# Chunked linear attention with two expert layers: the decay of the queries, the gate and ScalarE's late work are moved

## The chip, the cores and the metric

One core of a Trainium2 chip runs the whole program. The metric is the device time of one execution in microseconds (us). The engines are named as in the profile: PE is TensorE (PEld its weight loads), DVE is VectorE, ACT is ScalarE, POOL is GpSimd, SP is SyncE, which issues most DMAs.

## What is computed

Three layers follow one another: a linear attention with a decaying state, a mixture of eight experts with a greedy assignment under a capacity, and a dense layer of three products with a maximum. Only the attention and the gate's logits (`x @ w_gate`) bear on the change.

```python
def _attn_ref(r, k, v, w, u):                      # B, H, S, D = 4, 8, 768, 48
    for t in range(S):
        cur = einsum('bhd,bhe->bhde', u[None] * kt, vt)
        y[:, :, t] = einsum('bhd,bhde->bhe', rt, state + cur)
        state = w[None, :, :, None] * state + einsum('bhd,bhe->bhde', kt, vt)
def _moe_ref(x, w_gate, w1, w2):                   # 3072 tokens, 384 wide, 8 experts
    logits = x @ w_gate
    # greedy by logit, 384 tokens for each expert
    out[mask] = np.maximum(x[mask] @ w1[e], 0.0) @ w2[e]
# then: np.maximum(np.maximum(x @ v1, x @ v2), x @ v3) @ w_out
```

## The kernel before

The attention runs in 24 steps, one for each chunk of 128 tokens of one sequence: `steps` goes over the 6 chunks c, and inside over the 4 sequences b, so a sequence comes back every fourth step. Within a chunk the recurrence is turned into products: keys and queries are scaled by powers of the decay, the masked scores give the part of the chunk itself, and the state S of the sequence gives the part of the chunks before. Heads go in pairs, at partitions 0 to 47 and 64 to 111.

The order of the work is written out by hand in `Attention.run`: each engine takes its instructions in the order in which the program issues them. Step i issues, in this order: the loads for step i+4 (`load`), the transposed queries for i+3 (`across`), the storing of x of i-1 (`store`), all on SyncE's queue; GpSimd's decay of the queries of i+2 (`decayed`, L128, by the table `tr` in SBUF), its scaled keys of i+3 (`natural`, L183), its bonus products of i+2 (`bonus`, L191 and L192); then `turn` of i+2 (TensorE turns the keys, L212, ScalarE copies them out as `kt`, L214); `scores` of i+1 (TensorE L226, masked by VectorE as `am`, L229); `extra` of i+1 (VectorE sums the bonus, L200, GpSimd multiplies, L202); `cross` of i-1 (TensorE turns x into the bank `pX`, L297, ScalarE copies it out as `xt`, L299); `keep` (four products of constants, L236, whose result nobody reads); `rows` of i (TensorE L247, first against the state, then against the scores; VectorE adds the bonus into x, L262; ScalarE's Square of x with a sum, L263); `gate` of i-2 (three products with xt as the held operand, 8 columns, into 24 x 8 logits of one bank, L307); `state` of i (TensorE L281, VectorE's sum with the state, L285, and four copies by ScalarE that decay it, L289).

Between these lie four slots, `side(1)` to `side(4)`, in which the planner `Feed` issues the preparation of the expert weights: peaks by ScalarE's Square (L610), powers of two on VectorE, splits of each weight block into two half-precision parts by ScalarE (L677, L773) and VectorE (L681, L776), and the conversion of doubles (L717 to L748). The planner spreads its total cost evenly over the steps. What it has left is issued after the last step. Then the logits are negated into `raw` (L352), and the assignment of tokens and the expert products follow.

PSUM is full in this stage: one bank each for pT (turned keys), pX (x turned, also lent to the planner's small products), pK (state) and the logits, two each for pA (scores) and pY (rows).

Of the kernel before, what the change touches and what calls it, by code (L numbers as in the profile page):

```python
# [7 lines left out]
F32 = mybir.dt.float32  # L8
F16 = mybir.dt.float16
BF16 = mybir.dt.bfloat16  # L10
I32 = mybir.dt.int32
AF = mybir.ActivationFunctionType
# [6 lines left out]
C = 128  # L19
# [15 lines left out]
APART = 1.5  # L35
SLACK = (3.0, 2.0, 1.05, 2.0)
WARM = (20, 5, 14, 18)
KEEP = 4


def ap(t, offset, dims):
    return bass.AP(tensor=t.tensor, offset=t.offset + offset, ap=dims)


class Attention:


    def __init__(self, ctx, tc, K, r, rt, k, v, w, u, wg, x_dram, spare, routing):
        self.spare, self.routing = spare, routing
        self.tc, self.nc, self.K = tc, tc.nc, K  # L50
        self.r, self.rt, self.k, self.v, self.x_dram = r, rt, k, v, x_dram
        nc = self.nc
        self.loads = ctx.enter_context(tc.tile_pool(name="loads", bufs=5))
        self.work = ctx.enter_context(tc.tile_pool(name="work", bufs=2))
        self.tabs = ctx.enter_context(tc.tile_pool(name="tabs", bufs=1))
        self.psum = ctx.enter_context(tc.tile_pool(name="psum_a", bufs=1, space=PSUM))
        self.steps = [(b, c) for c in range(NC) for b in range(B)]
        self.LD, self.RN, self.KN, self.BV, self.RT, self.KT, self.AM, self.X, self.XT, self.RK = ({} for _ in range(10))
        wcol = self.tabs.tile([128, NP], F32, name="wcol")
        nc.vector.memset(wcol, 1.0)  # L60
        for s in range(2):
            nc.sync.dma_start(wcol[HALF[s]], ap(w, s * D, [[1, D], [R2, NP]]))
        self.RB, self.KB, self.KP = ([self.tabs.tile([128, NP * C], F32, name=f"{name}{j}") for j in range(m)]
                                     for name, m in (("rt", 4), ("kt", 2), ("kp", 4)))
        self.S = [self.tabs.tile([128, NP, WIDE], F32, name=f"S{b}") for b in range(B)]
        self.VB = [self.tabs.tile([128, DM + WIDE - D], F32, name=f"v{n}") for n in range(5)]
        nc.gpsimd.memset(self.RB[0], 0.0)
        self.load(0)
        self.across(0)
        for t in self.VB:  # L70
            nc.vector.memset(t[:, DM:], 0.0)
        self.K.identity()
        self.clear(self.KP[0])
        for t in self.RB[1:]:
            nc.gpsimd.memset(t, 0.0)
        for t in self.S:
            nc.gpsimd.memset(t[:, :, D:], 0.0)
        self.routing.fill()
        self.ub = self.tabs.tile([128, DM], F32, name="ub")
        nc.sync.dma_start(self.ub, ap(u, 0, [[0, 128], [1, DM]]))  # L80
        self.load(1)
        self.across(1)
        self.load(2)
        self.across(2)
        self.wg = self.tabs.tile([128, 3, E], F32, name="wg")
        nc.sync.dma_start(self.wg, ap(wg, 0, [[E, 128], [128 * E, 3], [1, E]]))
        self.tables(wcol)
        self.natural(1)
        self.natural(2)
        self.bonus(1)  # L90
        for i in range(2):
            self.decayed(i, nc.vector)
        self.bonus(0, nc.vector)
        self.fading()
        self.bank = self.psum.tile([128, 512], F32, name="lg")
        self.lg = self.bank[:, :NT * E].rearrange("p (m e) -> p m e", e=E)
        nc.tensor.matmul(self.bank[:, 256:], self.K.onesf.bitcast(BF16)[:, :128], self.K.onesf.bitcast(BF16), start=True, stop=True,
                         skip_group_check=True)

    def clear(self, t):  # L100

# [21 lines left out]
        for s in range(2):  # L123
            self.nc.sync.dma_start(t[HALF[s]], ap(self.rt, (b * NC + c) * C * DM + s * D * NP * C, [[NP * C, D], [1, NP * C]]))

    def decayed(self, i, engine=None):
        if i < NT:
            (engine or self.nc.gpsimd).tensor_mul(self.RT[i], self.RT[i], self.tr)  # L128

    def tables(self, wcol):  # L130
        nc, tabs, psum = self.nc, self.tabs, self.psum
        self.mask = tabs.tile([128, C], F32, name="mask")
        nc.gpsimd.memset(self.mask, 1.0)
        nc.gpsimd.affine_select(self.mask, self.mask, [[1, C]], OP.is_gt, 0.0, base=0, channel_multiplier=-1)
        scratch = [self.spare() for _ in range(2)]
        up, dn = (t[:, :NP * 65].rearrange("p (j n) -> p j n", n=65) for t in scratch)
        tk = scratch[0][:, 512:512 + NP * C].rearrange("p (j n) -> p j n", n=C)
        self.tr = tabs.tile([128, NP * C], F32, name="tr")
        tr = self.tr.rearrange("p (j n) -> p j n", n=C)
        nc.vector.memset(up[:, :, 0:1], 1.0)  # L140
        nc.vector.memset(dn[:, :, 64:65], 1.0)
        nc.vector.tensor_copy(up[:, :, 1], wcol)
        nc.vector.tensor_copy(dn[:, :, 63], wcol)
        pw = [wcol]
        n = 1
        while n < 64:
            p2 = tabs.tile([128, NP], F32, name=f"pw{2 * n}")
            nc.vector.tensor_mul(p2, pw[-1], pw[-1])
            b = pw[-1][:, :, None].to_broadcast([128, NP, n])
            nc.vector.tensor_mul(up[:, :, n + 1:2 * n + 1], up[:, :, 1:1 + n], b)  # L150
            nc.vector.tensor_mul(dn[:, :, 64 - 2 * n:64 - n], dn[:, :, 64 - n:64], b)
            pw.append(p2)
            n *= 2
        self.tkn = tabs.tile([128, H, 64], F32, name="tkn")
        for t in self.KP[1:]:
            self.clear(t)
        nc.scalar.activation(tk[:, :, :64], dn[:, :, 1:], AF.Copy)
        idle = psum.tile([128, 512], F32, name="pX")
        warm(nc, self.K, idle, WARM[0])
        for j in range(0, NP, 2):  # L160
            nc.vector.reciprocal(tk[:, j:j + 2, 64:], up[:, j:j + 2, 1:])
            p = psum.tile([128, 512], F32, name="pT")
            for n in range(2):
                nc.tensor.transpose(p[:, n * C:(n + 1) * C], tk[:, j + n, :], self.K.identf)
            warm(nc, self.K, idle, WARM[1])
            heads = slice(2 * j, 2 * j + 4)
            nc.scalar.activation(self.tkn[:, heads].rearrange("p h n -> p (h n)"), p[:, :2 * C], AF.Copy)
            self.natural(0, heads)
        nc.scalar.activation(tr[:, :, 64:], up[:, :, :64], AF.Copy)
        nc.vector.reciprocal(tr[:, :, :64], dn[:, :, :64])  # L170
        self.w64 = pw[-1]
# [57 lines left out]
            nc.vector.tensor_mul(am[:, s], pa[s], self.mask[:, None, :].to_broadcast([128, NP, C]))  # L229
        self.AM[i] = am  # L230

    def keep(self, n):

        ones = self.K.onesf.bitcast(BF16)
        for _ in range(n):
            self.nc.tensor.matmul(self.bank[:, 256:], ones[:, :128], ones, start=False, stop=True, skip_group_check=True)  # L236

    def rows(self, i):

        nc, psum = self.nc, self.psum  # L240
# [19 lines left out]
        parts = [t.rearrange("p (j s d) -> p j s d", j=NP, s=2) for t in (x, self.BV[i])]  # L260
        for s in range(2):
            nc.vector.tensor_add(parts[0][:, :, s], py[s][:, :, :D], parts[1][:, :, s])  # L262
        nc.scalar.activation(self.K.junk[:, :DM], x, AF.Square, accum_out=self.K.norms[:, i:i + 1])  # L263

    def store(self, i):
        if i >= 0:
# [4 lines left out]
    def state(self, i):  # L271
# [13 lines left out]
            nc.vector.tensor_add(t, pk[:, :, :D], S[:, :, :D])  # L285
        else:
            t = pk
        for j in range(NP):
            nc.scalar.activation(S[:, j, :D], t[:, j, :D], AF.Copy, scale=self.w128[:, j:j + 1])  # L289

    def cross(self, i):
        if i < 0:
            return
        nc, psum, work = self.nc, self.psum, self.work
        px = psum.tile([128, 3, C], F32, name="pX")
        for j in range(3):
            nc.tensor.transpose(px[:, j, :], self.X[i][:, j * 128:(j + 1) * 128], self.K.identf)  # L297
        xt = self.XT[i] = work.tile([128, 3, C], F32, name="xt", bufs=3)
        nc.scalar.activation(xt, px, AF.Copy)  # L299

    def gate(self, i):
        if i < 0:
            return
        b, c = self.steps[i]
        m = b * NC + c
        for j in range(3):
            self.nc.tensor.matmul(self.lg[:, m, :], self.XT[i][:, j, :], self.wg[:, j, :],  # L307
                                  start=(i == 0 and j == 0), stop=j == 2, skip_group_check=True)

    def run(self, feed):  # L310
        nc = self.nc
# [6 lines left out]
        for i in range(NT):  # L318
# [8 lines left out]
            self.load(i + 4)  # L327
            self.across(i + 3)
            self.store(i - 1)
            self.decayed(i + 2)  # L330
            self.natural(i + 3)
            self.bonus(i + 2)
            side(1)
            self.turn(i + 2)
            side(2)
            self.scores(i + 1)
            self.extra(i + 1)
            side(3)
            self.cross(i - 1)
            self.keep(KEEP)  # L340
            self.rows(i)
            self.gate(i - 2)
            side(4)
            self.state(i)
        while feed.left(9):
# [2 lines left out]
        self.gate(NT - 2)  # L348
        self.cross(NT - 1)
        self.gate(NT - 1)  # L350
        K = self.K
        nc.scalar.activation(K.raw, self.lg, AF.Copy, scale=-1.0)  # L352


class Consts:
# [1131 lines left out]
```

## Time and profile before

| | us |
|---|---|
| median of 3 runs | 698.33 |
| lowest and highest | 697.42, 699.98 |
| the profiled execution | 696.23 |
| its span in the profile | 694.5 |
| PE, DVE, ACT, POOL busy in the span | 644.6, 400.7, 351.5, 238.0 |

The busy times are sums over stages of very different kinds. The attention stage takes about the first 160 us, the assignment of tokens the 40 us after it, the expert and dense products the rest. So the page's totals say little of this change; views that are cut to the stage say more. In a waits view each row tells which engine and tile stood for which other engine and tile, in total, how often, and the longest. A busy PE includes short stalls inside a run of matmuls, since the ends of matmuls are modelled.

### The profile page before, as it was taken

How to read it: one execution, taken by the hardware profiler on the slowest of the kernel's cores; microseconds unless marked ns; L12 is line 12 of the kernel's file. 1: busy time of each engine (PE TensorE's matmuls, PEld its weight loads, DVE VectorE, ACT ScalarE, POOL GpSimd, SP SyncE). 2: the span in 40 equal slices, each digit the busy share in tenths (PEclk: the TensorE clock that was granted, in tenths of full speed). 3: DMA queues.
4: the chain of work that ended last, by engine and by line, in shares of the span. 5: the costliest groups of instructions: out<-in, count | busy, mean ns of one | idle time of the engine just before them, and what ended most of it. 6: DMA issues, size and time to landing. Idle time of an engine off the chain costs nothing.

```text
span 694.5 us, 14402 instructions
## 1 busy us (share of the span) xinstructions
PE 644.6 (93%) x5663; PEld 427.2 (62%) x5663; DVE 400.7 (58%) x1068; ACT 351.5 (51%) x785; POOL 238.0 (34%) x264
## 2 busy tenths in 40 slices
PE   7999998996599998699999999999999999999996
PEld 5788777875476554356666656666665666666663
DVE  7778897776725867646466455644636553451321
ACT  3766657643425556367466547446365536342321
POOL 6999999960050003113022112102212111110222
PEclk8999999995579999899999999999999999999999
DMA  7996757513034516016235211620612220000000
GB/s 220 315 295 216 246 186 250 162 37 103 2 107 139 172 42 194 22 68 160 68 103 108 98 57 30 170 75 35 160 45 74 45 89 1 35 0 1 36 1 34
DMA packets 54762, 72.97 MB, mean 105 GB/s; under 512 B 21408, under 2 KB 42016, under 8 KB 54688
## 3 DMA queue, kind: packets, MB, share of 16 engines
q1 hardware_dynamic: 51616, 62.55, 29.3%
q0 software_dynamic: 3072, 9.44, 4.7%
q8 instruction: 46, 0.75, 0.5%
q14 instruction: 28, 0.23, 0.1%
HBM read 58.41 MB, written 9.44 MB: 98 GB/s over the span
## 4 chain that ended last, share of the span: by engine, by line
PE 54%; issue 8%; DVE 5%; ACT 4%; POOL 1%; POOLq 0%; DVEq 0%; ACTq 0%
PE pg L897 25%; PE ps L897 20%; PE px L990 8%; ACT w L677 1%; DVE top L972 1%; POOL gt L977 1%; ACT junk L610 1%; DVE da L739 1%; DVE x2s L953 0%; ACT gt L976 0%; DVE ht L925 0%; DVE v L776 0%; DVE sc L423 0%; DVE da L732 0%; POOL out_dram L995 0%
## 5 line engine op out<-in xcount | busy, mean ns | idle before, releaser
L897 PE MATMUL pg<-x2s,v 128*128 128x384 f16 x1296 | 218.2, 326 | 5.3 <-ACT top L970 3.2
L897 PEld LDWEIGHTS <-v 128*128 128x128 f16 x1296 | 126.6, 98 | 90.9 <-issue 6.0
L977 POOL TENSOR_TENSOR gt<-top,gt 128x384 f16<-128x384 f32 x48 | 44.5, 928 | 349.2 <-ACT gt L976 295.5
L897 PEld LDWEIGHTS <-w 128*128 128x128 f16 x1242 | 116.8, 98 | 73.7 <-issue 2.3
L681 DVE SCALAR_TENSOR_TENSOR w<-stage,sc,w 128x512 f16<-128x512 f32 (+1 forms) x80 | 70.9, 906 | 61.1 <-ACT w L677 60.9
L972 DVE SCALAR_TENSOR_TENSOR top<-pg,sc,top 128x384 f32<-128x384 f32 x96 | 59.1, 615 | 74.4 <-PE pg L897 63.6
L897 PE MATMUL ps<-ht,w 128*128 128x384 f16 x576 | 94.9, 326 | 1.6 <-DVE ht L925 1.6
L897 PE MATMUL ps<-xt,w 128*128 128x384 f16 (+1 forms) x540 | 88.4, 317 | 0.2 <-ACT xt L888 0.2
L990 PE MATMUL px<-wo,gt 128*128 128x384 f16 x432 | 75.0, 334 | 6.9 <-DVE wo L776 3.0
L976 ACT ACTIVATE gt<-top 128x384 f16<-128x384 f32 x48 | 25.1, 523 | 109.5 <-DVE top L972 109.5
L990 PEld LDWEIGHTS <-gt 128*128 128x128 f16 x432 | 42.7, 100 | 38.1 <-issue 8.8
L677 ACT ACTIVATE w<-stage,sc 128x512 f16<-128x512 f32 (+1 forms) x80 | 61.6, 798 | 2.2 <-DVE sc L461 2.2
L610 ACT ACTIVATE junk<-stage 128x768 bf16<-128x768 f32 x64 | 53.7, 838 | 0.9
L925 DVE SCALAR_TENSOR_TENSOR ht<-ps,ht 128x384 f16<-128x384 f32 x56 | 31.0, 555 | 32.1 <-ACT ht L924 32.1
L995 POOL DMA_INDIRECT out_dram<-o,ids x24 | 23.9, 996 | 46.7 <-ACT o L993 46.7
L970 ACT ACTIVATE top<-pg,sc 128x384 f32<-128x384 f32 x48 | 27.6, 576 | 20.8 <-PE pg L897 18.3
L263 ACT ACTIVATE junk<-x 128x384 bf16<-128x384 f32 x24 | 12.6, 524 | 47.0 <-DVE x L262 44.7
L936 ACT ACTIVATE x<-ps 128x384 f32<-128x384 f32 x24 | 11.7, 490 | 47.0 <-PE ps L897 47.0
L924 ACT ACTIVATE ht<-ps 128x384 f16<-128x384 f32 x56 | 26.8, 482 | 15.9 <-PE ps L897 15.7
L993 ACT ACTIVATE o<-px,sc 128x384 f32<-128x384 f32 x24 | 13.9, 580 | 38.8 <-PE px L990 35.5
L229 DVE TENSOR_TENSOR am<-pA,mask 128x512 f32<-128x512 f32 x48 | 30.7, 681 | 4.3 <-PE pA L226 4.2
L128 POOL TENSOR_TENSOR rt<-rt,tr 128x512 f32<-128x512 f32 x22 | 31.4, 1427 | 0.2 <-DMA rt<-in_rt_dram 0.2
(231 smaller groups left out, 884.3 us busy)
## 6 DMA issues: line engine op xcount, KB each, us to landing
stage<-in_moe_w_dram SPq DMA_DIRECT2D x41, 768.0 KB, 5.6
kn<-in_k_dram SPq DMA_DIRECT2D x24, 192.0 KB, 4.9
rn<-in_r_dram SPq DMA_DIRECT2D x24, 192.0 KB, 5.0
v<-in_v_dram SPq DMA_DIRECT2D x24, 192.0 KB, 4.0
rt<-in_rt_dram SPq DMA_DIRECT2D x48, 96.0 KB, 3.5
x_rows<-x SPq DMA_DIRECT2D x24, 192.0 KB, 2.9
stage<-in_moe_w_out_dram SPq DMA_DIRECT2D x3, 768.0 KB, 4.4
xg<-x_rows,ids POOLq DMA_INDIRECT x24, 4.6
```

Source lines behind the costliest of these rows:

```text
L128: (engine or self.nc.gpsimd).tensor_mul(self.RT[i], self.RT[i], self.tr)
L229: nc.vector.tensor_mul(am[:, s], pa[s], self.mask[:, None, :].to_broadcast([128, NP, C]))
L610: self.nc.scalar.activation(self.K.junk, x, AF.Square, accum_out=total)
L677: nc.scalar.activation(hi, raw, AF.Copy, scale=st["s"])
L681: nc.vector.scalar_tensor_tensor(lo, raw, st["s"], hi, op0=OP.mult, op1=OP.subtract)
L897: nc.tensor.matmul(p[:, rows], w[:, wi, k, cols], x[:, xi, k, rows], start=k == 0 and wi + xi == 0, stop=k == kb - 1 and xi == 1, skip_gro ...
L924: nc.scalar.activation(h[:, 0, f], p, AF.Relu)
L925: nc.vector.scalar_tensor_tensor(h[:, 1, f], p, 0.0, h[:, 0, f], op0=OP.max, op1=OP.subtract)
L970: nc.scalar.activation(t, p, AF.Copy, scale=self.ratio[i])
L972: nc.vector.scalar_tensor_tensor(t, p, self.ratio[i], top, op0=OP.mult, op1=OP.max)
L977: nc.gpsimd.tensor_sub(gt[:, 1, g], top, gt[:, 0, g])
L990: nc.tensor.matmul(p, gt[:, gi, g, a * 128:(a + 1) * 128], self.WO[:, wi, g, :], start=g == 0 and gi + wi == 0, stop=g == self.KG - 1 and ...
```

## The change

The decay of the queries goes from GpSimd to VectorE, and later in the step; its table `tr` lies in PSUM, in the bank that held the logits. The products of constants go. The gate of chunk c is made for its four sequences at once, one chunk later: `gates` holds 32 columns of the gate's weights (8 used, the rest zero) and streams the turned x of each sequence into its own 32 partitions of pX; ScalarE copies that to `gs`, and `logits` turns it back by one product with four 8-column blocks of the identity, one step later. The last four steps keep the single gate, into the table's bank. Square moves from `rows` to `cross`, behind the copy of the turned x, and so one step later; the four copies of the state move from `state` into `fade`, issued in the next step behind `turn`. `xt` gets six buffers.

```diff
-KEEP = 4
+        self.ST = {}
-        self.wg = self.tabs.tile([128, 3, E], F32, name="wg")
-        nc.sync.dma_start(self.wg, ap(wg, 0, [[E, 128], [128 * E, 3], [1, E]]))
+        self.wg = self.tabs.tile([128, 3, 32], F32, name="wg")
+        nc.gpsimd.memset(self.wg, 0.0)
+        nc.sync.dma_start(self.wg[:, :, :E], ap(wg, 0, [[E, 128], [128 * E, 3], [1, E]]))
+        self.tr = self.psum.tile([128, 512], F32, name="lg")
+        self.raw = self.K.raw.rearrange("p (b c) e -> p b c e", b=B)
+        self.four = self.K.identf.rearrange("p (g n) -> p g n", n=32)
         self.tables(wcol)
...
-        self.bank = self.psum.tile([128, 512], F32, name="lg")
-        self.lg = self.bank[:, :NT * E].rearrange("p (m e) -> p m e", e=E)
-        nc.tensor.matmul(self.bank[:, 256:], ...)
...
-    def decayed(self, i, engine=None):
+    def decayed(self, i):
         if i < NT:
-            (engine or self.nc.gpsimd).tensor_mul(self.RT[i], self.RT[i], self.tr)
+            self.nc.vector.tensor_mul(self.RT[i], self.RT[i], self.tr)
...
-        self.tr = tabs.tile([128, NP * C], F32, name="tr")
...
-    def keep(self, n):
-        ones = self.K.onesf.bitcast(BF16)
-        for _ in range(n):
-            self.nc.tensor.matmul(self.bank[:, 256:], ones[:, :128], ones, start=False, stop=True, skip_group_check=True)
...
-        nc.scalar.activation(self.K.junk[:, :DM], x, AF.Square, accum_out=self.K.norms[:, i:i + 1])
...
-        for j in range(NP):
-            nc.scalar.activation(S[:, j, :D], t[:, j, :D], AF.Copy, scale=self.w128[:, j:j + 1])
+        self.ST[i] = t
+
+    def fade(self, i):
+        if i in self.ST:
+            for j in range(NP):
+                self.nc.scalar.activation(self.S[self.steps[i][0]][:, j, :D], self.ST[i][:, j, :D], AF.Copy,
+                                          scale=self.w128[:, j:j + 1])
...
-        xt = self.XT[i] = work.tile([128, 3, C], F32, name="xt", bufs=3)
+        xt = self.XT[i] = work.tile([128, 3, C], F32, name="xt", bufs=6)
         nc.scalar.activation(xt, px, AF.Copy)
+        nc.scalar.activation(self.K.junk[:, :DM], self.X[i], AF.Square, accum_out=self.K.norms[:, i:i + 1])
+
+    def gates(self, c):
+        nc = self.nc
+        p = self.psum.tile([128, 3, C], F32, name="pX")[:, 0]
+        for j in range(3):
+            for b in range(B):
+                nc.tensor.matmul(p[32 * b:32 * b + 32], self.wg[:, j], self.XT[c * B + b][:, j], start=j == 0, stop=j == 2,
+                                 skip_group_check=True)
+        self.GS = self.work.tile([128, C], F32, name="gs", bufs=1)
+        nc.scalar.activation(self.GS, p, AF.Copy)
+
+    def logits(self, c):
+        p = self.psum.tile([128, 3, C], F32, name="pX")[:, 0, :B * E]
+        self.nc.tensor.matmul(p, self.GS, self.four[:, :, :E], start=True, stop=True, skip_group_check=True)
+        self.settle(c, p)
 
     def gate(self, i):
-        ...
+        b = i % B
         for j in range(3):
-            self.nc.tensor.matmul(self.lg[:, m, :], self.XT[i][:, j, :], self.wg[:, j, :],
-                                  start=(i == 0 and j == 0), stop=j == 2, skip_group_check=True)
+            self.nc.tensor.matmul(self.tr[:, b * E:(b + 1) * E], self.XT[i][:, j], self.wg[:, j, :E], start=j == 0, stop=j == 2,
+                                  skip_group_check=True)
+
+    def settle(self, c, p):
+        self.nc.scalar.activation(self.raw[:, :, c], p.rearrange("p (b e) -> p b e", e=E), AF.Copy, scale=-1.0)
...
             self.store(i - 1)
-            self.decayed(i + 2)
             self.natural(i + 3)
             self.bonus(i + 2)
             side(1)
             self.turn(i + 2)
+            self.fade(i - 1)
             side(2)
             self.scores(i + 1)
             self.extra(i + 1)
+            self.decayed(i + 2)
             side(3)
             self.cross(i - 1)
-            self.keep(KEEP)
+            if i > B and i % B == 2:
+                self.logits(i // B - 1)
             self.rows(i)
-            self.gate(i - 2)
+            if i > B and i % B == 1:
+                self.gates(i // B - 1)
+            if i - 2 >= NT - B:
+                self.gate(i - 2)
             side(4)
             self.state(i)
...
-        nc.scalar.activation(K.raw, self.lg, AF.Copy, scale=-1.0)
+        self.settle(NC - 1, self.tr[:, :B * E])
```

## Rows read from the trace of the kernel before

**Rows 1.** TensorE in order of time: first and 21st transposes of x (start, us, instruction).

```profile
22.64 0.55 PE L297 MATMUL pX<-identf,x 128*128 128x128 f32 x3
...
144.15 0.55 PE L297 MATMUL pX<-identf,x 128*128 128x128 f32 x3
```

**Rows 2.** Busy by stretch: length, PE, PEld, DVE, ACT, POOL, granted clock, DMA, GB/s.

```profile
22.60:144.20 121.60, 114.88 (x2160) 98.27 (x2158) 99.00 (x192) 81.19 (x217) 119.83 (x102) 0.99 0.70 225
144.20:160.10 15.90, 13.67 (x264) 11.91 (x262) 9.73 (x18) 6.11 (x15) 6.33 (x6) 0.99 0.18 54
...
100.00:110.00 10.00, 9.52 (x191) 7.98 (x189) 10.00 (x17) 6.15 (x18) 9.84 (x8) 1.00 0.69 223
```

**Rows 3.** Who waited for whom, 22.6 to 144.2 us: us in total, times, longest.

```profile
PE pT L212 <- POOL kp L183: 5.7, 6, 1.6
...
DVE sc L758 <- ACT junk L610: 4.1, 2, 2.2
...
DVE da L732 <- ACT da L717: 2.2, 2, 1.6
DVE x L262 <- POOL kp L183: 2.1, 3, 0.8
DVE sc L659 <- ACT junk L610: 2.1, 3, 1.4
DVE v L776 <- ACT v L773: 1.6, 3, 0.7
DVE x L262 <- POOL rt L128: 1.5, 3, 0.8
DVE w L681 <- ACT w L677: 1.4, 3, 0.5
...
ACT junk L263 <- DVE x L262: 35.0, 20, 4.5
```

**Rows 4.** GpSimd's groups of instructions, same stretch: count, busy us, mean ns, idle before.

```profile
L128 POOL TENSOR_TENSOR rt<-rt,tr 128x512 f32<-128x512 f32 x20 | 28.4, 1420 | 0.2 <-DMA rt<-in_rt_dram 0.2
```

**Rows 5.** TensorE in order of time through one step: start, us, instruction.

```profile
90.27 0.55 PE L297 MATMUL pX<-identf,x 128*128 128x128 f32 x3 [0.19 <-DVE sc L447]
90.65 0.60 PE L236 MATMUL lg<-onesf 128*128 128x256 bf16 x4
91.18 0.69 PE L247 MATMUL pY<-S,rt 64*64 64x64 f32 x32
...
92.89 0.83 PE L307 MATMUL lg<-wg,xt 128*128 128x8 f32 x6
93.65 0.69 PE L281 MATMUL pK<-v,kp 128*64 128x64 f32 x16
...
94.86 1.16 PE L226 MATMUL pA<-rt,kt 64*128 64x128 f32 x16
95.95 0.55 PE L297 MATMUL pX<-identf,x 128*128 128x128 f32 x3
```

**Rows 6.** Instructions of lines 229 and 128 on VectorE: min/median/max ns, first and last start.

```profile
L229 DVE TENSOR_TENSOR am<-pA,mask x46: 674/680/692, 18.4 to 152.3; 128x512 f32<-128x512 f32 x46
...
L128 DVE TENSOR_TENSOR rt<-rt,tr x2: 694/776/859, 10.6 to 11.9; 128x512 f32<-128x512 f32 x2
```

**Rows 7.** TensorE's weight loads: who waited for whom, 22.6 to 144.2 us.

```profile
PEld pY L247 <- issue: 4.4, 21, 0.2
```

**Rows 8.** ScalarE's copy of the turned x, and SyncE's DMA of the gate's weights.

```profile
92.41 0.47 ACT L299 ACTIVATE xt<-pX 128x384 f32<-128x384 f32 x1
...
11.03 0.40 SPq L86 DMA_DIRECT2D wg<-in_moe_w_gate_dram  x1
```

**Rows 9.** TensorE around its longest hole, and the stretch after the hole.

```profile
68.71 0.55 PE L297 MATMUL pX<-identf,x 128*128 128x128 f32 x3
...
77.44 0.69 PE L297 MATMUL pX<-identf,x 128*128 128x128 f32 x3
...
74.38:77.79 3.41, 3.40 (x22) 2.85 (x23) 3.41 (x6) 1.98 (x7) 3.33 (x3) 0.50 0.68 180
```

More of the change, by code (lines that the diff above doesn't have):

```diff
@@ L91, in __init__ @@
         for i in range(2):
-            self.decayed(i, nc.vector)
+            self.decayed(i)
         self.bonus(0, nc.vector)
         self.fading()
-        self.bank = self.psum.tile([128, 512], F32, name="lg")
-        self.lg = self.bank[:, :NT * E].rearrange("p (m e) -> p m e", e=E)
-        nc.tensor.matmul(self.bank[:, 256:], self.K.onesf.bitcast(BF16)[:, :128], self.K.onesf.bitcast(BF16), start=True, stop=True,
-                         skip_group_check=True)
     def clear(self, t):
@@ L297, in cross @@
             nc.tensor.transpose(px[:, j, :], self.X[i][:, j * 128:(j + 1) * 128], self.K.identf)
-        xt = self.XT[i] = work.tile([128, 3, C], F32, name="xt", bufs=3)
+        xt = self.XT[i] = work.tile([128, 3, C], F32, name="xt", bufs=6)
         nc.scalar.activation(xt, px, AF.Copy)
+        nc.scalar.activation(self.K.junk[:, :DM], self.X[i], AF.Square, accum_out=self.K.norms[:, i:i + 1])
[12 more added lines that the diff above has]
+        self.settle(c, p)
     def gate(self, i):
[L302 to L305, printed above, removed]
+        b = i % B
         for j in range(3):
-            self.nc.tensor.matmul(self.lg[:, m, :], self.XT[i][:, j, :], self.wg[:, j, :],
-                                  start=(i == 0 and j == 0), stop=j == 2, skip_group_check=True)
+            self.nc.tensor.matmul(self.tr[:, b * E:(b + 1) * E], self.XT[i][:, j], self.wg[:, j, :E], start=j == 0, stop=j == 2,
+                                  skip_group_check=True)
+    def settle(self, c, p):
+        self.nc.scalar.activation(self.raw[:, :, c], p.rearrange("p (b e) -> p b e", e=E), AF.Copy, scale=-1.0)
     def run(self, feed):
@@ L350, in run @@
         self.gate(NT - 1)
-        K = self.K
-        nc.scalar.activation(K.raw, self.lg, AF.Copy, scale=-1.0)
+        self.settle(NC - 1, self.tr[:, :B * E])
 class Consts:
```

## Prediction

> **What bounds the kernel now.** Only the attention stage is touched, so I read the split of the span into stretches first, then who waits for whom inside the stage, then one step of TensorE in order of time. From the first transposes of x to those of step 21 the trace holds 121.5 us for 20 steps, 6.08 us each [rows 1]. In that stretch (22.6 to 144.2 us) GpSimd is busy 119.83 of 121.60 us, TensorE 114.88, VectorE 99.00, ScalarE 81.19; the last 15.9 us, the tail, hold little GpSimd work [rows 2]. GpSimd is without work for 1.8 us in all, and TensorE's longest waits are for GpSimd's scaled keys (5.7 us in 6 times, one of 1.6) [rows 3]. So GpSimd sets the pace: five products of a step take 119.83 / 20 = 6.0 us, and one of them, the decay of the queries, is 1.42 us of that [rows 4]. The next engine is close behind: one step that did not wait runs on TensorE from 90.27 to 95.95, 5.68 us without a hole in it [rows 5]. VectorE stands idle 22.6 us of the stretch, 11.4 of them for ScalarE in the weight preparation (five rows) and 3.6 for GpSimd's bonus rows; ScalarE itself spends 35.0 us standing in front of the Square, which waits for VectorE's x while everything behind it in ScalarE's queue waits too [rows 3].
>
> **The change, part by part.** *GpSimd* loses the decay: 6.0 - 1.42 = 4.6 us a step. It no longer sets the pace.
>
> *VectorE* gains the decay. Its nearest row is the masking of the scores, 128x512 f32, one operand in PSUM and one in SBUF, just as the decay will have (its result goes to SBUF too): 674 to 692 ns over 46 of them. The same product with both operands in SBUF ran twice on VectorE, 694 and 859 ns [rows 6]. I take 0.68 (same operands), with 0.86 as the upper bound. 20 x 0.68 = 13.6 us, so VectorE has 99.0 + 13.6 = 112.6 us of work in a stretch that now lasts 121.6. It becomes the fullest engine. (Upper bound: 20 x 0.86 = 17.2, that is 116.2.) The lower bound is the work alone, 112.6; less than that would need the weight preparation to run faster beside a less busy GpSimd, for which I take nothing. Behind the decay in VectorE's queue stand x and the state's sum. x may be late: after the rows' products TensorE has the state, the turning of the keys and the scores to do before it wants x, 93.65 to 95.95 = 2.3 us [rows 5]. Without that cover each decay would cost its 0.68 on the path. The decay needs the queries' DMA, issued a step earlier as before and now used later in the step, so no wait is added.
>
> *TensorE* loses the constants' products, 90.65 to 91.18 = 0.53 us, and the gate of each step, 92.89 to 93.65 = 0.76 us [rows 5]: 5.68 - 1.29 = 4.39 us. Every fourth step it gains the gate in fours: 12 products, each two records as the gate's 3 products are 6 records now. Bounds for the 24: 24 x 0.022 (the state's part of the rows, 32 in 0.69 us) = 0.5 us, and 24 x 0.127 (the gate now, 6 in 0.76) = 3.0 us. I take the scores' 0.068 (16 in 1.09), which also stream 128 columns and share the array: 1.6 us. The turning back is one more product, 0.25 us. Per step (1.6 + 0.25) / 4 = 0.46, so 4.85 us; with the bounds 4.6 to 5.2. That is below VectorE's 112.6 / 20 = 5.6.
>
> A switch of the array's split shows today: 21 times the weight load of the quarter-array products stands 0.2 us for nothing else that the profile shows [rows 7]. TensorEngine Tiling of the Trainium skill (Key Properties) says that changing the tiling mode drains TensorE, which speaks against a gate cut into 32-column strips between other shapes. By that rule two more switches come in each of five steps, 5 x 2 x 0.2 = 2 us of TensorE's time in all; by the bare count of products, none. TensorE has 20 x (5.6 - 4.85) = 15 us to spare, so either way the sum below is the same.
>
> *The new waits on TensorE.* Both the gate in fours and its turning back use the one bank of the x transposes, so they wait until ScalarE has copied the transposes out. In the gate step the rows' products, 1.7 us, lie between and cover it. In the turning step nothing does: the product stands directly behind the transposes, and the rows, the state and the next scores queue behind it. ScalarE's copy of transposes begun at 90.27 ran from 92.41 to 92.88 [rows 5, 8]; TensorE would have stood 90.65 to 92.88 = 2.2 us. The least is the copy alone, 0.5 us. Since Square no longer blocks ScalarE I take 1.2 us, five times. It falls in the 0.75 us a step that TensorE has to spare, and I count 0.5 us each, 2.5 us, as idle time of VectorE (ends 0 and 2.2, in sum 0 and 11).
>
> *ScalarE* gets Square behind the copy of the transposes, and the four copies of the state behind the next step's keys. Both then wait for things long done: the 11.4 us that VectorE stands for ScalarE should go, and the 3.6 for GpSimd too. The state's sum has one buffer and waits for the four copies, which now lie 2 to 3 us ahead of it in the same step; at c = 0 the next state's bank waits in the same way. Ten short copies are added, bounded by the transposes' 0.47 [rows 8]: 4.7 us of ScalarE at most, against 40 us in which it is idle.
>
> *Set-up and end.* The gate's weights are cleared on GpSimd before their DMA; that DMA is issued at 11.03 [rows 8], and GpSimd clears the tile ahead of the mask that the first step needs, so SyncE's queue does not wait. The table is written to PSUM instead of SBUF, by the same two instructions: nothing. In the tail three sets of constants go, 3 x 0.53 = 1.6 us, but the tail keeps its single gates and takes one gate in fours; I count 1 us. The last Square lies beside the last gate: nothing, at most its 0.7 us.
>
> **The sum.** Of VectorE's idle 22.6 us, 15.0 should go; of the other 7.6, which wait mostly for TensorE, I keep 1.5, because a VectorE that is behind finds TensorE's results ready. 112.6 + 1.5 + 2.5 = 116.6 us against 121.6: -5.0. With the tail -6.0. The rest of the kernel moves with it. The profiled execution took 696.23 us (694.5 of span, 1.73 around it) and would take 690.2; the median of the runs is 2.1 us above that execution, so **692.3 us**. About 0.5%, 3.5 us, is what a measurement can tell from no change.
>
> **Rivals.** *A: TensorE stops at the turning back and its clock falls (slower).* For: the one hole of 1.6 us in the stretch [rows 3] was followed by 3.41 us at a granted clock of 0.50, that is 1.2 in place of 2.4 GHz, and the transposes before and after lie 77.44 - 68.71 = 8.7 us apart where 5.7 is the undisturbed step [rows 9]: 3.0 us lost for one hole. The constants' products that filled TensorE are gone. Five holes of 2.2 us, the clock falling each time, cost 2.2 + 1.7 (3.41 us at half speed) = 3.9 us, 19.5 in all, against 8.5 us of gain without the holes: 698.3 + 11 = 709 if nothing is absorbed, and about 704 if the spare 0.75 us of a step and its neighbour absorb 1 us each time. It decides from some 2.4 us a time: 5 x 2.4 = 12 eats the 8.5 and 3.5 more. Against: that hole came of GpSimd, as all 5.7 us of such waits did [rows 3], and GpSimd is then out of the way.
>
> *B: VectorE is full and nothing is won.* All of the 7.6 us stay, the decay costs 0.86, the turning back 1 us a time: 116.2 + 7.6 + 5 = 128.8 at the worst, with 0.68 it is 125.2; with half the idle gone, 121.4, less 1 in the tail: 697 us, between 695 and 702. For: in-order queues seldom run full. Against: from 100 to 110 us VectorE ran 10.00 of 10.00 [rows 2].
>
> *C: VectorE runs full.* 112.6 and no idle, the tail less 1.6 to 3: -10.6 to -12, 687 us; with some relief from a freer GpSimd 684. It is the lower end of the forecast.
>
> *D: the gain is lost later.* After the stage only a chain of short instructions and the expert products follow, planned anew from the end of attention; they move with it. I give this 2 in 100, inside B.
>
> **How the numbers follow.** The forecast (with C) 0.60, B 0.23, A 0.17. Forecast and C lie between 684 and 694.8; B between 695 and 702; A above. The range that leaves out no more than 2 in 10 takes in the forecast, C and B: 684 to 702. The forecast's own range is 687 to 695. Faster 0.60, same 0.23, slower 0.17.
>
> **What the profile will show.** Right: GpSimd with waits in every step and its 22 decays gone; 24 decays on VectorE at 0.68 us; VectorE over 94% busy in the stretch; nearly nothing of ScalarE's 35 us in front of Square; steps of 5.7 to 5.9 us with at most a few longer ones where the gate is turned back. Wrong: the decay above 0.75 us; TensorE idle behind the copy of the transposes for over 1.5 us each fourth step; stretches at half clock inside the stage; or VectorE with over 8 us of idle time, for TensorE this time.

## The result, and the profile after

The changed kernel takes 704.56 us (median of 7 runs, 702.23 to 705.78) against 698.33 for the kernel before: 6 us slower by the medians, where 692.3 was forecast. The ratio on record is 1.0063, 95% interval 1.0040 to 1.0086; it is not the quotient of the two medians, which is 1.0089, and makes the loss 4.4 us. The time lies outside the range that was given. It lies 0.6 us above the 704 that rival A priced, and that rival had a chance of 0.17.

The attention stage holds nearly the whole loss. The profiled executions took 704.56 and 696.23 us. The logits are complete at 167.5 us of the one against 160.1 of the other, 7.4 us later; from there to the end it is 535 us against 534. About half of the loss comes late in the stage. From the first set of transposes of x to the 21st (22.27 to 147.91 us) it is 125.64 us against 121.51 before [rows 1]; from there to the logits, in the tail, it is 19.63 against 15.95, where the forecast counted a gain of 1 us. First the busy time by stretch (length, then busy us of PE, PEld, DVE, ACT and POOL, the granted clock, the DMA share, GB/s), the two stretches of the stage and then three single steps, from one set of transposes of x to the next:

```profile
22.60:144.20 121.60, 99.12 (x1980) 83.19 (x1979) 105.31 (x205) 78.54 (x217) 89.16 (x79) 0.90 0.69 223
144.20:167.70 23.50, 20.09 (x357) 17.20 (x356) 14.10 (x26) 9.64 (x26) 5.78 (x6) 0.78 0.14 45
...
20.00:167.54 147.54, 121.68 (x2371) 102.44 (x2365) 121.28 (x234) 90.48 (x247) 97.46 (x87) 0.88 0.61 196
...
106.27:115.00 8.73, 6.64 (x105) 5.71 (x105) 7.82 (x13) 5.53 (x18) 5.39 (x6) 0.62 0.54 171
65.41:73.16 7.75, 5.04 (x106) 4.30 (x104) 7.75 (x12) 2.72 (x8) 5.12 (x4) 0.92 0.82 270
61.08:65.41 4.33, 4.33 (x106) 3.74 (x104) 4.23 (x7) 4.08 (x9) 4.11 (x5) 1.00 0.67 196
```

Set beside [rows 2], GpSimd has fallen from 119.83 to 89.16 us of the same stretch and sets no pace any more; VectorE has risen from 99.00 to 105.31; the clock has fallen from 0.99 to 0.90. And the steps have come apart. An undisturbed step is now 4.33 us, against the 5.68 of [rows 5]. But a step with much weight preparation is 7.75 us, all of it VectorE's, and one with a turning back of the gate is 8.73 us, with the clock at half speed for much of it.

Who waited for whom from 20 to 165 us (us in total, times, longest), TensorE's rows, then VectorE's and ScalarE's:

```profile
PE pX L312 <- ACT xt L296: 7.4, 5, 2.1
PE pA L225 <- issue: 5.1, 2, 2.7
PE pX L417 <- ACT xt L296: 4.5, 3, 3.1
PE pA L225 <- DVE rt L128: 3.6, 2, 1.9
...
PE pX L305 <- ACT xt L296: 1.4, 1, 1.4
...
DVE x L255 <- PE pY L240: 5.5, 2, 4.6
...
ACT junk L629 <- DVE wo L767: 18.3, 6, 5.5
ACT kt L213 <- PE pT L211: 9.6, 6, 3.0
ACT xt L296 <- PE pX L294: 8.8, 3, 4.9
ACT S L285 <- DVE st L277: 7.4, 5, 4.2
```

L312 is the turning back of the gate, L305 the gate in fours, L417 a small product of the planner, L225 the scores' products. The waits for GpSimd of [rows 3] are gone, and three others stand in their place: TensorE waits for ScalarE's copy of the turned x wherever something else wants that bank (7.4 + 4.5 + 1.4 us), and the scores wait for the decay in VectorE's queue (3.6 us, and most likely the 5.1 that the profile puts to no engine, since VectorE is full there and `early` below, which moves the decay alone, has no such row). ScalarE lost its 35.0 us in front of Square, and 44.1 us of waits in front of other work stand in the four rows shown.

One turning back in order of time, TensorE first, then ScalarE:

```profile
106.27 0.88 PE L294 MATMUL pX<-identf,x 128*128 128x128 f32 x3 [0.59 <-DVE x L255]
109.23 0.64 PE L312 MATMUL pX<-identf,gs 128*128 128x32 f32 x2 [2.09 <-ACT xt L296]
109.80 1.13 PE L240 MATMUL pY<-S,rt 64*64 64x64 f32 x32
...
105.69 0.84 ACT L629 ACTIVATE junk<-wo 128x768 bf16<-128x768 f32 x1 [3.89 <-DVE wo L767]
...
107.33 0.58 ACT L213 ACTIVATE kt<-pT 128x512 f32<-128x512 f32 x1
107.81 1.00 ACT L285 ACTIVATE S<-st,w 128x48 f32<-128x48 f32 x4
108.71 0.47 ACT L296 ACTIVATE xt<-pX 128x384 f32<-128x384 f32 x1
```

The transposes end by 107.2. ScalarE had stood 3.89 us for VectorE's bits of the weights (`wo`) until 105.69, and is still at the keys and at the four copies of the state, which the change puts ahead of the copy of x, and gets to it at 108.71. TensorE stands 2.09 us for it, with a product of 0.4 to 0.6 us at the head of its queue and the rows of the step behind.

### The profile page after: what moved, and what is told of

It is laid out like the page before. It is cut to its first block, busy times and chain, and to the rows that moved or that the text cites. A ratio compares the mean times of both kernels' runs of the same rounds, so it can differ in the third digit from the quotient of the medians.

```text
span 702.8 us, 14238 instructions
## 1 busy us (share of the span) xinstructions
PE 635.2 (90%) x5576; PEld 418.0 (59%) x5576; DVE 410.7 (58%) x1090; ACT 352.9 (50%) x795; POOL 205.5 (29%) x243
## 4 chain that ended last, share of the span: by engine, by line
PE 53%; issue 8%; DVE 5%; ACT 4%; POOL 1%; POOLq 0%; DVEq 0%; ACTq 0%
PE pg L916 25%; PE ps L916 20%; PE px L1009 8%; ACT w L696 1%; DVE top L991 1%; POOL gt L996 1%; ACT junk L629 1%; DVE da L758 1%; DVE x2s L972 0%; ACT gt L995 0%; DVE ht L944 0%; DVE v L795 0%; DVE sc L442 0%; DVE da L751 0%; POOL out_dram L1014 0%
## 5 line engine op out<-in xcount | busy, mean ns | idle before, releaser
L629 ACT ACTIVATE junk<-stage 128x768 bf16<-128x768 f32 x64 | 53.6, 838 | 5.9 <-DMA stage<-in_moe_w_dram 5.0
L225 PE MATMUL pA<-rt,kt 64*128 64x128 f32 x384 | 31.1, 301 | 9.5 <-issue 5.1
L989 ACT ACTIVATE top<-pg,sc 128x384 f32<-128x384 f32 x48 | 27.7, 576 | 20.8 <-PE pg L916 18.3
L182 POOL TENSOR_TENSOR kp<-kn,tkn 128x384 f32<-128x384 f32 (+1 forms) x25 | 29.4, 1178 | 17.5 <-PE pK L273 12.4
L225 PEld LDWEIGHTS pA<-rt,kt 64*128 64x128 f32 x384 | 26.2, 201 | 13.6 <-issue 7.3
```

The costliest lines, as they stand in the source:

```text
L182: self.nc.gpsimd.tensor_mul(self.KN[i][:, heads, :D], kn[:, heads], self.tkn[:, heads, :D])
L225: nc.tensor.matmul(pa[s][:, j, :], kt[FULL[s], j * C:(j + 1) * C], rt[FULL[s], j * C:(j + 1) * C], start=True, stop=True, skip_group_check ...
L629: self.nc.scalar.activation(self.K.junk, x, AF.Square, accum_out=total)
L989: nc.scalar.activation(t, p, AF.Copy, scale=self.ratio[i])
```

## The experiments

Theory 1: the stop at the turning back is the loss. Theory 2: VectorE is full, and TensorE waits for it. Theory 3: the clock falls because the products of constants are gone. All ratios are against runs of the kernel before on the same chip. Time at half clock is twice what the mean granted clock lacks of 1, times the stretch from 20 us to the last logits; for the changed kernel 2 x 0.12 x 147.5 = 35 us, for the kernel before 3 to 4 us. The figures below are read from finer stretches and can differ by 1 or 2 us from the mean that is shown.

**A place of its own for the gate (`own`).**

```diff
+        self.half = self.psum.tile([128, 512], F32, name="pK")
-        p = self.psum.tile([128, 3, C], F32, name="pX")[:, 0]            # gates
+        p = self.half[:, 256:384]
-        p = self.psum.tile([128, 3, C], F32, name="pX")[:, 0, :B * E]    # logits
+        p = self.half[:, 384:384 + B * E]
-        pk = psum.tile([128, NP, WIDE], F32, name="pK")
+        pk = self.half[:, :NP * WIDE].rearrange("p (j n) -> p j n", n=WIDE)
```

> The changed kernel, with the gate in fours and its turning back in a free half of the state's bank instead of the bank of the turned x, so that neither waits for ScalarE's copy of the turned x. Theory 1 (the stop at the turning back, and the clock that falls after it, cost the time): the 7.4 us of waits at the turning back and the 1.4 at the gate go, the half-clock time of the stage (34 us) falls below 25, and the time goes from 704.6 to about 697. Theory 2 (VectorE is full in the steps with much weight preparation, and TensorE waits for it): the waits move to the scores' products, the time stays at 702 or more. Theory 3 (the clock falls for lack of the constants' products, wherever the holes are): half-clock time stays near 30 us, about 702.

696.95 us, ratio 0.9969 (0.9947 to 0.9992). TensorE's waits from 20 to 165 us:

```profile
PE pA L226 <- issue: 5.9, 3, 2.7
PE pX L418 <- DVE x L256: 3.2, 1, 3.2
PE pK L274 <- ACT gs L309: 2.1, 4, 0.9
PE pA L226 <- DVE rt L129: 1.9, 1, 1.9
...
PE pK L313 <- DVE st L278: 0.5, 1, 0.5
```

At the turning back (here L313) one wait of 0.5 us is left; 2.1 us of a wait of the next state for the copy of the gate have come, since these now share a bank. The half-clock time only fell to 27 us, and yet 7 us are back. That is theory 1, with the part about the clock left open.

**The constants put back (`keep`).**

```diff
             self.cross(i - 1)
+            self.keep(KEEP)      # four products, 256 columns, in a free half of a pY bank
             if i > B and i % B == 2:
```

> The changed kernel, with the four products of constants put back behind the turned x in every step (in a free half of a rows bank). Theory 3: half-clock time in the stage falls from 34 us to under 10 and the time to about 697. Theory 1: the constants fill 0.5 us of each stop, the rest of the stop stays, 702 to 705. Theory 2: the holes in TensorE stay where VectorE is late, half-clock time 20 to 30 us, 703 to 706.

700.82 us, 1.0010 (0.9983 to 1.0038), half-clock time 10 us. The stops stay (6.0 us in five waits for ScalarE's copy, in the profile of its fastest run, 696.66 us). Neither theory takes all: while the stops are there, the constants give back some 0.5%, less than theory 3 forecast and more than theory 1 allowed for.

**Both (`ownkeep`).**

> Both: own place for the gate in fours and the constants put back. If theories 1 and 3 together are the cause: half-clock time under 7 us and 692 to 696, below the kernel before. Theory 2: holes for VectorE stay, 699 or more.

698.86 us, 0.9999 (0.9971 to 1.0026), half-clock time 7 us. A miss for theories 1 and 3 together, and 0.1 us from the 699 that theory 2 named: with the stops gone the constants win nothing. They are themselves 0.53 us of TensorE's time in each step [rows 5]. So this does not say that half clock costs nothing, only that the faster clock gives back no more than that work takes.

**The decay back on GpSimd (`pool`).**

```diff
+        self.tr = self.tabs.tile([128, NP * C], F32, name="tr")       # SBUF, not PSUM
             self.store(i - 1)
+            self.decayed(i + 2)                                       # GpSimd
             ...
             self.extra(i + 1)
-            self.decayed(i + 2)                                       # VectorE
```

> The changed kernel with the decay of the queries alone undone: on GpSimd at its old place, its table in SBUF. Theory 2: VectorE loses 15 us of work, the waits of the scores for it go, GpSimd sets 6.0 us a step again, 698 to 700. Theory 1: the stops at the turning back stay, 7 us or more of them, and the time is 704 or more.

701.89 us, 1.0017 (0.9985 to 1.0048), between both expectations: 8.6 us of stops at the gate stay as theory 1 says, and TensorE waits 12.4 us for GpSimd's keys again.

**One line moved: the turning back behind the rows (`late`).**

```diff
             self.cross(i - 1)
-            if i > B and i % B == 2:
-                self.logits(i // B - 1)
             self.rows(i)
+            if i > B and i % B == 2:
+                self.logits(i // B - 1)
```

> The changed kernel with one line moved: the turning back of the gate stands behind the rows' products instead of ahead of them, in the same bank. Theory 1 (the stop directly behind the turned x is the loss): the 7.4 us of waits there fall under 2, and the time is 696 to 699, as with a bank of its own. Rival (it was the sharing of the bank with the planner's small products, or the gate itself, that cost): 702 or more.

695.35 us, 0.9928 (0.9893 to 0.9962): 9 us under the changed kernel by a line's place, and clearly below the kernel before. TensorE in order of time at the same turning back, and the stage's row:

```profile
104.43 0.72 PE L294 MATMUL pX<-identf,x 128*128 128x128 f32 x3 [0.59 <-DVE x L255]
105.08 1.13 PE L240 MATMUL pY<-S,rt 64*64 64x64 f32 x32
106.14 1.97 PE L240 MATMUL pY<-v,am 128*64 128x64 f32 x32
108.05 0.41 PE L312 MATMUL pX<-identf,gs 128*128 128x32 f32 x2
...
20.00:158.80 138.80, 119.66 (x2357) 100.23 (x2357) 121.46 (x233) 89.65 (x246) 96.09 (x87) 0.90 0.65 208
```

The rows' products follow the transposes at once, even at half clock as here, and by their end the bank is long free. The clock's mean is 0.90, as in `own`.

Step by step the two profiles show where the stops cost time. A step runs from one set of transposes to the next; its granted clock stands in brackets:

| turning back | stop, us | step, changed kernel | step, `late` | difference |
|---|---|---|---|---|
| 1 | 1.09 | 6.49 (1.00) | 5.68 (1.00) | 0.81 |
| 2 | 1.82 | 6.52 (1.00) | 4.82 (1.00) | 1.70 |
| 3 | 2.09 | 8.73 (0.62) | 6.33 (0.73) | 2.40 |
| 4 | 1.85 | 8.03 (0.79) | 5.38 (1.00) | 2.65 |
| 5 | 0.58 | 6.28 (0.50) | 4.52 (0.62) | 1.76 |

A neighbour makes good most of the second and third: the step ahead of the second takes 7.98 us against 9.88 in `late`, the step behind the third 4.84 against 6.33. From the first transposes to the logits the changed kernel takes 145.27 us against 136.94. Of these 8.3 us, 2.3 have come by the 16th set of transposes, behind the third turning back, and 6.0 come after it. Set against `own` it is 2.1 and 5.3 us.

At the last turning back the clock costs more than the stop itself. Its step and the next one, in the changed kernel (first the stop) and then in `late`, with the columns of the first view above:

```profile
155.63 0.63 PE L312 MATMUL pX<-identf,gs 128*128 128x32 f32 x2 [0.58 <-ACT xt L296]
...
154.18:160.46 6.28, 5.70 (x75) 5.00 (x76) 3.45 (x7) 1.19 (x4) 0.83 (x1) 0.50 0.09 34
160.46:165.57 5.11, 5.11 (x81) 4.58 (x81) 0.66 (x3) 0.99 (x3) 0.00 (x0) 0.64 0.10 38
...
148.78:153.30 4.52, 4.52 (x76) 3.96 (x76) 3.45 (x7) 1.19 (x4) 0.83 (x1) 0.62 0.13 47
153.30:156.82 3.52, 3.52 (x81) 3.21 (x81) 0.66 (x3) 0.99 (x3) 0.00 (x0) 1.00 0.15 56
```

The two steps take 11.39 us against 8.04, 3.35 more, with a stop of 0.58. VectorE works only 4.11 us of them; TensorE is busy 10.81 us against 8.04 with the same products. So 2.8 of the 3.35 us are TensorE's own work at a lower clock, and nothing hides them. In both kernels the clock falls about where the step begins, behind waits for VectorE (1.73 and 0.32 us); in `late` it is back at 1.00 in the next step, in the changed kernel, where TensorE stops once more, it is not.

**The parts of the change alone, on the kernel before.** `vec`: the decay on VectorE, at the change's place, table in PSUM (logits and constants move to free halves of banks). `act`: Square behind the copy of x, the state's copies one step later. `vecact`: both. `fours`: the gate in fours and its turning back in line, all else as before.

```diff
# vec
-            self.decayed(i + 2)                    # GpSimd, behind store
+            self.decayed(i + 2)                    # VectorE, behind extra
# act
-        nc.scalar.activation(self.K.junk[:, :DM], x, AF.Square, ...)          # rows
+        nc.scalar.activation(self.K.junk[:, :DM], self.X[i], AF.Square, ...)  # cross
+            self.fade(i - 1)                                                  # behind turn
# fours
             self.keep(KEEP)
+            if i > B and i % B == 2:
+                self.logits(i // B - 1)
             self.rows(i)
-            self.gate(i - 2)
+            if i > B and i % B == 1:
+                self.gates(i // B - 1)
+            if i - 2 >= NT - B:
+                self.gate(i - 2)
```

> The kernel before with one part of the change alone: the decay of the queries on VectorE, behind the bonus sum, table in PSUM; single gates, constants, ScalarE's order as before (logits and constants move into free halves of other banks). If a fuller VectorE is worth nothing (theory 2): VectorE over 120 us busy in a stage that stays at 139 to 141 us, 697 to 701. If GpSimd's pace was the whole bound, as forecast: 5.7 us a step, 690 to 694.

> The kernel before with ScalarE's part alone: Square behind the copy of the turned x, the state's copies one step later. GpSimd keeps its 6.0 us a step, so 697 to 700 if GpSimd's pace is the bound; VectorE's 10 us of waits for ScalarE should fall under 4 in either case. If those waits were on the path: 690 to 694.

> The kernel before with both parts, the decay on VectorE and ScalarE's order, single gates and constants kept: the change without the gate in fours. Theory 1: no stop at a turning back, no fall of the clock, 696 to 699, as with the gate in a place of its own. The forecast's sum without the gate's part: 692 to 695.

> The kernel before with the third part of the change alone: the gate in fours and its turning back in line, in the bank of the turned x; single decay on GpSimd, constants and ScalarE's order as before. If the stop at the turning back is the loss by itself (theory 1): with ScalarE held by Square it is as long or longer than in the change, 1.5 to 2.5 us five times, 704 to 710. If it only costs where VectorE is the fullest engine: 697 to 701, since GpSimd's pace hides it.

| kernel | us | ratio | 95% interval |
|---|---|---|---|
| `vec` | 700.54 | 1.0029 | 1.0007 to 1.0050 |
| `act` | 696.87 | 0.9976 | 0.9956 to 0.9996 |
| `vecact` | 695.08 | 0.9955 | 0.9922 to 0.9988 |
| `fours` | 705.08 | 1.0066 | 1.0044 to 1.0088 |

`vec` was to win most by the forecast, and loses 0.3%: undisturbed steps stay at 5.68 us, TensorE's own time with single gates and constants, and ScalarE now stands 50.7 us in front of Square. `act` wins a little, though GpSimd's pace is untouched; together they give 3 us, though the intervals of `act` and `vecact` overlap. `fours` alone is as slow as the whole change, with the constants in place and about 11 us at half clock. Its waits on TensorE, 20 to 165 us (L316 the turning back, L309 the gate in fours, L299 the turned x):

```profile
PE pX L316 <- ACT xt L301: 6.6, 4, 2.4
PE pT L214 <- POOL kp L185: 4.0, 4, 1.9
PE pX L309 <- ACT xt L301: 3.8, 3, 2.0
PE pX L299 <- ACT gs L312: 2.7, 2, 1.4
```

13.1 us of waits round one bank, and 4.0 us of the GpSimd waits left, where [rows 3] has 5.7. That GpSimd's pace would hide them, the other expectation, fell.

**What holds the kernel with the turning back moved: `latealt`, `latekeep`, `lateearly`.** All start from `late`. `latealt` gives every second decay back to GpSimd, with a copy of the table in SBUF; `latekeep` puts the constants back; `lateearly` moves the decay:

```diff
             side(2)
+            self.decayed(i + 2)
             self.scores(i + 1)
             self.extra(i + 1)
-            self.decayed(i + 2)
```

> The changed kernel with the turning back behind the rows, and every second decay back on GpSimd (a copy of the table in SBUF). Theory 2 (what is left to lose is that VectorE is full in the steps with much weight preparation): VectorE has 7 us less, GpSimd 5.3 us a step, the scores' waits for VectorE (9.4 us with the turning back moved alone) fall by half, 690 to 694. If VectorE is not what holds the stage: 695 to 697.

693.86 us, 0.9907 (0.9871 to 0.9943), as expected of a VectorE that is too full: the scores' waits fell from 9.4 to 4.3 us. The time is not clear of `late`, since the intervals overlap.

> The changed kernel with the turning back behind the rows, and the four products of constants put back in every step. If the falls of the clock still cost (27 us at half clock with the turning back moved alone): half-clock time under 10 us and 690 to 693. If a slow TensorE costs nothing where VectorE is full, and the constants only take its time: 696 to 699.

696.47 us, 0.9954 (0.9934 to 0.9974), half-clock time down from 27 to 10 us and no time won: the faster clock gives back no more than the work of the constants takes.

> The changed kernel with the turning back behind the rows, and the decay issued ahead of the masking of the scores instead of behind the bonus sum, 1.8 us earlier in VectorE's queue. If the scores' products wait for the decay's place in the queue: their 9.4 us of waits halve, 691 to 694. If they wait because VectorE is full as a whole: the waits go over to other rows, 695 to 698.

690.70 us, 0.9884 (0.9832 to 0.9936), the fastest of all. Its waits on TensorE and its stage:

```profile
PE pA L225 <- DVE am L228: 4.1, 5, 1.7
PE pX L417 <- ACT xt L296: 4.1, 3, 3.0
PE pX L294 <- DVE x L255: 3.1, 5, 0.8
...
20.00:154.73 134.73, 119.32 (x2371) 99.48 (x2365) 117.75 (x233) 89.64 (x247) 99.96 (x87) 0.92 0.67 214
```

The 9.4 us of `late` in which the scores waited (3.9 for the decay, 5.5 put to no engine) have become 4.1 for the masks.

**The decay's place by itself (`early`), and the constants once more (`lateearlykeep`).** `early` is the changed kernel with the last diff alone.

> The changed kernel with the decay alone moved ahead of the masking of the scores; the turning back stays in line behind the turned x. If the stop at the turning back is the whole loss: over 5 us of waits there stay and the time stays above the kernel before, 700 to 703. If the decay's late place carried as much of it: the scores' waits for VectorE go and the time falls under the kernel before, 694 to 698.

697.27 us, 0.9993 (0.9969 to 1.0016): the second expectation. The stops are there, 9.6 us of them, and still the loss is gone, though the time is not clearly under the kernel before:

```profile
PE pX L312 <- ACT xt L296: 6.5, 5, 2.4
PE pX L305 <- ACT xt L296: 3.1, 2, 2.2
PE pA L225 <- DVE am L228: 3.0, 4, 0.9
```

> The changed kernel with the turning back behind the rows, the decay ahead of the masks, and the products of constants put back in every step. If the 20 us at half clock that are left without them cost time: under 10 us at half clock and 686 to 689. If they cost nothing because TensorE then has time to spare, and the constants only add work: 691 to 695.

693.59 us, 0.9921 (0.9888 to 0.9954), half-clock time 7 us: the constants cost, here as in `own` and `late`, some 0.3% each time. The intervals of each pair overlap; that all three point one way is what there is.

So the loss of the changed kernel has two parts. Moving the turning back wins 1.0063 - 0.9928 = 1.35%, 9.4 us, with the decay late, and 0.9993 - 0.9884 = 1.09%, 7.6 us, with the decay early. Moving the decay wins 0.70%, 4.9 us, with the stop in line; without it 0.44%, 3.1 us, which the intervals do not separate from nothing. Either alone is enough to bring the kernel back to the time before or under it. With the decay early the stops cost time in the same places: `early` takes 0.9 us more than `lateearly` up to the 16th set of transposes, and 5.2 more from there to the logits. With both moved, the 20 steps take 117.44 us in `lateearly`, where the forecast's sum was 116.6.

## Why the prediction was wrong, point by point

- *GpSimd's pace and its end*: right. Its work fell to 89 us of the stretch and TensorE waits for it no more.
- *The decay at 0.68 us on VectorE*: right, 674 ns, 669 to 689 over 22. VectorE's busy time over the stage rose by 11.7 us (109.58 to 121.28), less than the 22 x 0.674 = 14.8 added, since some of its other work ran shorter (the bit work of L732, now L751, 1038 to 795 ns on average; whether the freer GpSimd is the reason was not tested).
- *TensorE's step*: right. 4.39 was worked out, 4.33 is what an undisturbed step takes. The gate in fours took 0.79 us for its 24 records, from 100.59 to 101.38, half of the 1.6 that was taken and within its bounds. The Trainium skill (TensorEngine Tiling (Array Packing), Key Properties) says that a change of the tiling mode drains TensorE. All that the trace has for it behind the gate in fours is three holes of 0.2 us at most in the weight loads of the state, nothing to the sum.
- ***The step that failed: "I count 0.5 us each, 2.5 us, as idle time of VectorE"* for the stops at the turning back.** The stop itself was sized well enough, 1.2 us forecast and 7.4 / 5 = 1.5 measured, 2.1 the longest. What failed is the price of it. Moving the stops away gives back 7.6 to 9.4 us, 1.5 to 1.9 each, in place of 0.5. The reason given, 0.75 us of spare TensorE time in every step, was a mean over steps that do not share their spare time. At the first three turning backs, among steps of 7 or 8 us that VectorE fills, the price was not far off: 2.3 us up to the 16th set of transposes (2.1 and 0.9 in the other two pairs), against 1.5 forecast. From there on, with two turning backs, it was 6.0 us (5.3 and 5.2). TensorE has hardly any time to spare in those steps, busy 4.96 of 5.38 and 4.52 of 4.52 us in `late`, and its clock fell or stayed low, for which the sum had no term; at the last turning back that alone is 2.8 us. These are single executions; that three pairs divide alike is what speaks for it.
- *VectorE's idle time*, the same error in the sum's own terms: 1.5 + 2.5 us were counted over the 20 steps. VectorE's work was near the forecast, 109.36 us for 112.6, but it stood 125.64 - 109.36 = 16.3 us, 9.1 of them for TensorE by the profile. The reason for the 1.5, that a VectorE that is behind finds TensorE's results ready, does not hold where TensorE itself is behind.
- *The tail*: wrong. A gain of 1 us was counted and 3.7 us were lost (19.63 us against 15.95). The clock's mean is 0.74 there. With the constants back in line (`keep`), where they fill the last stop, the tail takes 15.73 us at 1.00; with the turning back and the decay moved and no constants (`lateearly`), 15.31 at 1.00.
- *"No wait is added"* by the decay, said of the queries' DMA: VectorE stood 1.0 us for that, once. The wait that was overlooked is another. On GpSimd it stood first in the step; on VectorE it stands behind the masks and the bonus sum, and where VectorE is late the next scores wait for it. 3 to 5 us, a term that the sum lacked.
- *ScalarE freed*: half right. Square's 35 us went, and VectorE's waits for ScalarE fell to 2.6 us. But ScalarE stands as long elsewhere, above all 18.3 us for the planner's bits (L629), and in the turning back shown that made it late for x again.
- *Rival A*: right in its place and in both its parts, with too small a chance. That its time, 704, came out is partly luck. It took 19.5 - 5 = 14.5 us for the five holes and their clock, where moving them gives back 7.6 to 9.4, and nothing for the decay's place, which took 3 to 5. Its 8.5 us of gain without the holes was good: `lateearly` is 1.16% or 8.1 us under the kernel before.
- *Rival B*: its time is that of `own` and `ownkeep` (696.95 and 698.86), but `late` and `lateearly` (695.35 and 690.70) show that a full VectorE is not the end of it.

Not settled: how the loss at all five turning backs splits between the stop's own length and the clock that falls after it. With the constants in place, and 10 or 7 us at half clock, moving the stops away wins 1.0010 - 0.9999 = 0.1% (`ownkeep`) or 1.0010 - 0.9954 = 0.6% (`latekeep`); without them 0.9% (`own`) or 1.35% (`late`). So some 0.8%, 5 to 6 us, comes only of stops and missing constants together. Not all of that need be the clock's, since constants that run inside a stop, 0.53 us each time, do not lengthen it. Only at the last turning back do the rows part the two.

## What to carry to other kernels

A product that reuses a bank waits for the copy out of that bank, and on an in-order engine all behind it waits too; put such a product behind other work of the same step, or give it half a bank that is free, before counting on spare time elsewhere. Spare time taken as a mean over steps is not there in the steps where the wait falls: read the longest and the shortest step before pricing a stop, and price the last steps by themselves. Work that goes over to another engine takes that engine's place in line, so ask what stands ahead of it there in the fullest step.

## What the runs showed that was not expected

Putting the constants back removed 13 to 20 us at half clock from the stage, and the time rose by about 0.3% in each of three pairs in which TensorE did not stop at the turning back. That sets the work of the constants against a faster clock, and the balance differs within the stage. Over the 20 steps, where VectorE is the fullest engine, `own` takes 121.49 us and `ownkeep` 122.55; in the tail, where it is not, 16.35 and 15.32. `late` and `latekeep` differ in the same way (120.66 and 123.84, then 16.28 and 15.25). And 24 records of the gate cut into four strips of 32 columns took 33 ns each, where the single gate's took 127 [rows 5]. Whether that is because the strips run beside each other, or because 32 columns are held in place of 128, no run separates.
